# Scores of two attention units in one visit to TensorE, and first output products set ahead of a statistics step

## The chip, the cores and the metric

One core of one Trainium2 chip. The metric is the device time of one execution in microseconds (us). Engines: PE is TensorE (PEld is its weight load), DVE is VectorE, ACT is ScalarE, POOL is GpSimd, SP is SyncE, which issues the DMAs. The granted clock is the share of full speed (2.4 GHz) that TensorE got in a stretch; its other level is 1.2 GHz.

## The reference, cut to what matters

```python
# attention: q, k, v are (4, 8, 576, 64); heads 0-3 see the last 32 positions, heads 4-7 every 32nd position
scores = np.where(masks, q @ k.T / 8, -1e9)
attn = exp(scores - max); attn = attn / (attn.sum() + 1e-9)
x = (attn @ v) reordered to (2304, 512)
# first feed-forward block, with a norm in front
xn = x / sqrt(mean(x * x) + 1e-6) * rms_g
x = (silu(xn @ w_gate) * (xn @ w_val)) @ w_out      # 512 -> 1536 -> 512
# second block
return softplus(x @ w_in) @ w_out2                  # 512 -> 2048 -> 512
```

Everything is float32 outside.

## The kernel before, in words

**Order.** The kernel does not issue its instructions as it meets them. Each is put down with `pr.add(engine, estimated cost, closure, reads, writes)`; a planner (`Program.emit`, `Trial.run`) then lists all of them in an order made from those estimates, the dependencies and due times. `emit` is called twice: once for attention and ten of the twelve steps of block 1's first side, once for the rest. So what the program text gives is dependencies; the order on each engine is the planner's, and an engine then runs its list strictly in that order.

**Attention.** The work is cut in 32 units. A unit is one batch, one pair of heads (p = 0, 1 local, p = 2, 3 strided) and 4 to 6 blocks `a` of queries; two units in a row (u even, u odd) are the two parts of one pair of heads, loaded together (`load`). `stage_s(u)` makes the scores of a unit in one PSUM bank: a bf16 product that writes the mask (L540), then per block and head a 64 by 64 float32 product (L546), 96 columns wide for local units and 54 for strided ones. Head h lies in rows 64h to 64h + 63 of the operands, and its scores go to partitions 64h to 64h + 63 of the bank, so the two heads of a unit use two opposite quarters of the 128 by 128 array: (rows 0-63, columns 0-63) and (rows 64-127, columns 64-127). A float32 product is two PE instructions in the profile. Then VectorE takes the maximum (L558). For units 0 to 15 ScalarE does the exponentials from the bank (L576); for units 16 to 31 VectorE subtracts first (L560) and ScalarE does one exponential (L573). `stage_t` transposes the probabilities (L614), `stage_v` multiplies with the values (L637). There, the two units of a strided pair have their keys in rows 0-53 and 64-117, and their two heads in the two column halves, and `values` puts both units' products down together.

**Units 0 to 15** run in `attend`, with PE, ScalarE and VectorE all at work. The scores have four banks (`q_banks`) up to unit 11; from step 12 (`early`) two (`s_banks`), as `f_banks` then takes the first gate and value products. `at_step(17, prepare, 1, (0,), ...)` starts the preparation of step 1's gate and value weights.

**Units 16 to 31** are dealt out among the steps of block 1 (`steps`, four units at a time, two banks), between the feed-forward products L434.

**Between the two** come, in program order: `half(1, 0)` (gate and value of step 1, tokens 0-511, 24 products), `stats(1)` (sums of squares L453, Ln and Exp L457/L458, three VectorE steps, `norm`), a load of ScalarE's Silu table, `chain1` for (0, 0) and (1, 0) (Silu L844, product L845, a split in two float32r parts L833/L355), `direct(1)` (splits of the normed tokens 512-1023 for the products), and `half(0, 1)`. The first output products `out1` for tokens 0-511 (`outs1(1, True, (0, 1))`, four calls of six products L434 and one ScalarE copy L876) come later, with those for tokens 512-1023, after step 1.

Of the kernel before, what the change touches and what calls it, by code (L numbers as in the profile page):

```python
# [18 lines left out]
EXP_LN = "natural_log_exp_and_others"  # L19
# [6 lines left out]
KD = DM // 128  # L26
# [6 lines left out]
QW = 608  # L33
# [4 lines left out]
DEALT = 10  # L38
# [209 lines left out]
def attn_glu_softplus(  # L248
# [16 lines left out]
    def all_of(key):  # L265
        return (key, 0, 1 << 30)
# [211 lines left out]
    def attention(at, use):  # L478
# [18 lines left out]
        for b in range(B):  # L497
            for p in (0, 2, 1, 3):
                units += [(b, p, 0, 5), (b, p, 5, 4)] if p < 2 else [(b, p, 0, 6), (b, p, 6, 5)]
        probs, trans, vals, ld, both, scored = {}, {}, {}, {}, {}, {}  # L500

        def load(u, b, p, n):
            loc = p < 2
# [17 lines left out]
        def load_v(u):  # L521
# [4 lines left out]
            vals[u // 2] = (vt, kv)  # L526
            dma(nt * (48 if p < 2 else 50), lambda: nc.sync.dma_start(out=vt[:kp, :nt, :], in_=src), [], [all_of(kv)])

        def stage_s(u):
            b, p, t0, n = units[u]  # L530
            loc = p < 2
            nk, st = (LK, 64) if loc else (SK, SK)
            if t0 == 0:
                load(u, b, p, n)
            qt, kq = ld[u // 2]
            sp, kb_ = use.s.next()
            m0 = 64 + ((5 - n) * LK if loc else 5 * LK)
            for h in range(2):
                r = slice(64 * h, 64 * h + 64)
                pr.add("PE", n * nk / 4.8 + 10, lambda r=r: nc.tensor.matmul(  # L540
                    sp[r, :n * nk], lhsT=mask[r, :64], rhs=mask[r, m0:m0 + n * nk], start=True, stop=False,
                    skip_group_check=True), [all_of("mask")], [kb_], mode=3)
            for a in range(n):
                for h in range(2):
                    r, x = slice(64 * h, 64 * h + 64), (t0 + a) * st
                    pr.add("PE", 83 if loc else 54, lambda a=a, h=h, r=r, x=x: nc.tensor.matmul(  # L546
                        sp[r, a * nk:(a + 1) * nk], lhsT=qt[r, x:x + 64], rhs=qt[r, QW + x:QW + x + nk],
                        start=False, stop=True, skip_group_check=True),
                        [(kq, t0 + a, t0 + a + 1), (kq, t0 + a + 100, t0 + a + 101)]
                        + [all_of("id")] * (u == 1), [kb_], mode=3)  # L550
            sv = sp[:, :n * nk].rearrange("p (a c) -> p a c", c=nk)
            e, ke = eb.next()
            e = e[:, :n * nk]
            ev = e.rearrange("p (a c) -> p a c", c=nk)
            z, kz = mz.next()
            m, z = z[:, 0, :n], z[:, 1, :n]
            km, kz = (kz[0], 10, 20), (kz[0], 0, 10)
            dve(n * nk, lambda: nc.vector.reduce_max(out=m, in_=sv, axis=AX.X), [kb_], [km])  # L558
            if whole(u):
                dve(n * nk, lambda: nc.vector.tensor_sub(ev, sv, m.unsqueeze(2).to_broadcast([128, n, nk])),  # L560
                    [kb_, km], [ke])
            else:
                dve(6, lambda: nc.vector.tensor_scalar(out=m, in0=m, scalar1=-SCALE, scalar2=None, op0=ALU.mult),
                    [km], [km])
            scored[u] = (e, ke, ev, z, kz, sv, kb_, m, km)
# [58 lines left out]
        def stage_v(u):  # L624
            b, p, t0, n = units[u]
            loc = p < 2
            r0, r1 = (0, LK) if loc else (64, 64 + SK) if t0 else (0, SK)
            v0 = t0 if loc else 0
            vt, kv = vals[u // 2]
            pts = trans.pop(u)  # L630
            nq = 64 if loc else SK
            xb, kx = use.v.next()
            for a in range(n):
                t, kt = pts[a // 3]
                for h in range(2):
                    o = (2 * (a % 3) + h) * nq
                    pr.add("PE", 59, lambda a=a, h=h, o=o, t=t: nc.tensor.matmul(  # L637
                        xb[64 * h:64 * h + 64, a * nq:(a + 1) * nq], lhsT=vt[r0:r1, v0 + a, 64 * h:64 * h + 64],
                        rhs=t[r0:r1, o:o + nq], start=True, stop=True), [all_of(kv), kt],
                        [kx], mode=1 if loc else 3)  # L640
            g = rg_sb[:, p:p + 1]
            if loc:
                c0 = b * S + 64 * t0
                w = 64 * n
                lo, hi = c0, c0 + w
                src = xb[:, :w]

                def tokens(x, x0, a0, a1):
                    return x[:, a0 - x0:a1 - x0]

                def mine(x, a0, a1):
                    return x[:, a0 - lo:a1 - lo]
            else:
                cls = min(3 * n, 32 - 3 * t0)
                w = cls * 18
                lo, hi = b * S, (b + 1) * S
                src = xb[:, :w].rearrange("p (c m) -> p c m", m=18)

                def tokens(x, x0, a0, a1):
                    return x[:, a0 - x0:a1 - x0].rearrange("p (m c) -> p c m", c=32)[:, 3 * t0:3 * t0 + cls, :]  # L660

                def mine(x, a0, a1):
                    return x[:, :, (a0 - lo) // 32:(a1 - lo) // 32]
            kss = ("ssq", lo, hi)
            for a0, a1 in ((lo, min(hi, TA)), (max(lo, TA), hi)):
                if a0 >= a1:
                    continue
                m = w * (a1 - a0) // (hi - lo)
                y = tokens(sview(a0, a1), a0, a0, a1)
                z = mine(src, a0, a1)  # L670
                kss = ("ssq", a0, a1)
                if a1 <= TA:
                    x, kxs = xview(p, a0, a1)
                    evict(m, tokens(x, a0, a0, a1), z, [kx], [kxs])
                    continue
                if p == 0:
                    act(m, lambda y=y, z=z: nc.scalar.activation(y, z, AF.Square), [kx], [kss])
                else:
                    s2, k2 = sq.next()
                    s2 = s2[:, :m] if loc else s2[:, :m].rearrange("p (c m) -> p c m", m=(a1 - a0) // 32)  # L680
                    act(m, lambda s2=s2, z=z: nc.scalar.activation(s2, z, AF.Square), [kx], [k2])
                    two("POOL", m, "tensor_add", y, y, s2, [kss, k2], [kss])
                x, kxs = xview(p, a0, a1)
                evict(m, tokens(x, a0, a0, a1), z, [kx, all_of("rg")], [kxs], g)
# [270 lines left out]
    with tc.manual_schedule():  # L955
# [6 lines left out]
        def at_step(u, fn, *args):  # L962
            plan.setdefault(u, []).append((fn, args))
# [22 lines left out]

        at_step(HOLD[0] + 3, prepare, 0, (0, 1), HOLD[0])
        at_step(12, early)
        at_step(17, prepare, 1, (0,), HOLD[1])

        def fill(u):
            pr.side = True
# [18 lines left out]

        def side_a(f, queue):

            if f and f != DEALT:
                prep1(f, 0, (0, 1) if f > 1 else (1,))
            w = w_at(f, 0)
            for c in (0, 1) if f > 1 else (1,):
                gate, val = gates.pop((f, c), (None, None))
                gate = gate or plain(w, 0, c, f_banks)
                step(queue)  # L1020
                drain(1)
                val = val or plain(w, 1, c, f_banks)
                step(queue)
                g[f, c] = chain1(gate, val, eng="DVE" if f < DEALT else "POOL")
                drain(1 if f < W1N - 1 else 0)
                step(queue)
            if f % 2:
                todo.extend(outs1(f, f == 1, (0, 1)))

        with ExitStack() as c2:  # L1030
            use = SimpleNamespace(s=q_banks, t=t_banks, v=v_banks)
            x = attention(c2.enter_context(tc.tile_pool(name="at", bufs=1)), use)
            attend(x, fill)
            pr.side = True
            half(1, 0, s_banks)
            pr.side = False
            stats(1, t_banks)
            table("silu_and_others")
            for f in (0, 1):
                g[f, 0] = chain1(*gates.pop((f, 0)))  # L1040
            direct(1)
            half(0, 1, v_banks)
            tv = Ring(banks.t[2:4], "bank", 2)
            use.t = use.v = tv
            for i in (0, 1):
                fk["gv"].keys[len(fk["gv"].t)] = ("ssq", i * CH, i * CH + CH)
                fk["gv"].t.append(ssq[:, i * CH:i * CH + CH])
            queue, last_turn = steps(x, {1: (2,)}, tv)
            o_banks.t = banks.t[4:6]
            for f in range(DEALT):  # L1050
                side_a(f, queue)
            step(queue, len(queue))
            prep1(DEALT, 0)
            pr.emit()
# [131 lines left out]
```

## Time and profile before

| | |
|---|---|
| Median of three runs | 910.92 us (910.21 to 915.23) |
| The profiled execution | 912.66 us, its span 910.9 us |
| PE busy | 893.4 us of the span |
| DVE busy | 717.1 us |
| ACT busy | 484.6 us |
| POOL busy | 21.7 us |
| Granted clock, mean | 0.994 |

The span is the time from the first to the last instruction; the run's own time has 1.8 us more around it. Matmuls are pipelined and overlap, so a busy PE is not a PE at its peak; the distance between the starts of two instructions says what one costs in a row of them.

### The profile page before, as it was taken

How to read it: one execution, taken by the hardware profiler on the slowest of the kernel's cores; microseconds unless marked ns; L12 is line 12 of the kernel's file. 1: busy time of each engine (PE TensorE's matmuls, PEld its weight loads, DVE VectorE, ACT ScalarE, POOL GpSimd, SP SyncE). 2: the span in 40 equal slices, each digit the busy share in tenths (PEclk: the TensorE clock that was granted, in tenths of full speed). 3: DMA queues.
4: the chain of work that ended last, by engine and by line, in shares of the span. 5: the costliest groups of instructions: out<-in, count | busy, mean ns of one | idle time of the engine just before them, and what ended most of it. 6: DMA issues, size and time to landing. Idle time of an engine off the chain costs nothing.

```text
span 910.9 us, 14075 instructions
## 1 busy us (share of the span) xinstructions
PE 893.4 (98%) x5320; PEld 736.5 (81%) x5320; DVE 717.1 (79%) x1358; ACT 484.6 (53%) x992; POOL 21.7 (2%) x22
## 2 busy tenths in 40 slices
PE   8888999999999999999999999999999999999998
PEld 7666787778778788888888888888888888888886
DVE  5979888898589995888988799886699556676645
ACT  6967664535355566545445568544473764343331
POOL 0001000000000000000000000000000000000000
PEclk9999999999999999999999999999999999999999
DMA  8865666262240263345544006331114111101003
GB/s 262 271 190 158 214 196 202 99 193 88 82 128 23 81 196 105 104 139 162 179 145 128 24 24 216 118 104 46 47 47 139 48 47 47 46 24 45 2 1 116
DMA packets 41859, 102.19 MB, mean 112 GB/s; under 512 B 4800, under 2 KB 5568, under 8 KB 41792
## 3 DMA queue, kind: packets, MB, share of 16 engines
q1 hardware_dynamic: 41792, 101.31, 35.1%
q8 instruction: 41, 0.67, 0.3%
q14 instruction: 26, 0.21, 0.1%
HBM read 78.74 MB, written 22.54 MB: 111 GB/s over the span
## 4 chain that ended last, share of the span: by engine, by line
PE 66%; DVE 3%; issue 0%
PE bank L434 66%; DVE xs L878 1%; DVE ob L355 0%; DVE tb L355 0%; DVE xs L355 0%; DVE win L355 0%; DVE w L355 0%; DVE ssq L355 0%; DVE glx L355 0%; DVE xs L896 0%; DVE gv L355 0%; DVE gv L845 0%; DVE ssq L845 0%; DVE gl L355 0%
## 5 line engine op out<-in xcount | busy, mean ns | idle before, releaser
L434 PE MATMUL bank<-ob,win 128*128 128x512 f32 (+1 forms) x1560 | 436.0, 363 | 4.5 <-ACT ob L351 2.5
L434 PEld LDWEIGHTS bank<-ob,win 128*128 128x128 f32 x1560 | 285.7, 189 | 57.9 <-ACT ob L351 2.7
L434 PE MATMUL bank<-tb,win 128*128 128x512 f32 x672 | 232.9, 392 | 0.0
L434 PEld LDWEIGHTS bank<-tb,win 128*128 128x128 f32 x672 | 125.4, 188 | 22.9 <-DVE xs L878 0.4
L896 DVE TENSOR_TENSOR xs<-bank,xs 128x512 f32<-128x512 f32 x126 | 87.0, 691 | 45.6 <-PE bank L434 44.3
L405 ACT ACTIVATE win<-w 128x512 fp32r<-128x512 f32 (+1 forms) x136 | 83.5, 617 | 64.0 <-PE bank L434 37.2
L434 PE MATMUL bank<-wout,ghx 128*128 128x512 f32 x304 | 100.0, 390 | 0.0
L355 DVE TENSOR_TENSOR win<-w,win 128x512 fp32r<-128x512 f32 (+1 forms) x132 | 87.8, 671 | 14.7 <-ACT win L405 11.5
L434 PE MATMUL bank<-wout,gh 128*128 128x512 f32 x272 | 90.4, 390 | 0.0
L434 PE MATMUL bank<-ghx,wout 128*128 128x512 f32 x224 | 84.1, 394 | 0.0
L434 PE MATMUL bank<-gh,wout 128*128 128x512 f32 (+1 forms) x256 | 81.6, 354 | 0.5 <-DVE xs L878 0.4
L878 DVE TENSOR_TENSOR xs<-bank,xs 128x512 f32<-128x512 f32 (+1 forms) x100 | 62.7, 632 | 11.0 <-PE bank L434 10.1
L434 PEld LDWEIGHTS bank<-wout,ghx 128*128 128x128 f32 x304 | 56.9, 188 | 11.7
L434 PEld LDWEIGHTS bank<-wout,gh 128*128 128x128 f32 x272 | 50.9, 188 | 10.5
L793 ACT ACTIVATE gv<-bank 128x512 f32<-128x512 f32 x48 | 28.5, 593 | 47.8 <-PE bank L434 47.2
L434 PE MATMUL bank<-wout,glx 128*128 128x512 f32 x152 | 53.1, 389 | 0.0
L434 PEld LDWEIGHTS bank<-gh,wout 128*128 128x128 f32 x256 | 45.5, 189 | 8.2 <-DVE xs L878 1.4
L434 PEld LDWEIGHTS bank<-ghx,wout 128*128 128x128 f32 x224 | 41.9, 188 | 8.4 <-ACT ghx L833 0.2
L434 PE MATMUL bank<-wout,gl 128*128 128x512 f32 x136 | 47.7, 389 | 0.0
L373 DVE SCALAR_TENSOR_TENSOR cvu<-raw,cvu 128x512 uint32<-128x512 uint32 x68 | 46.8, 688 | 0.9
L355 DVE TENSOR_TENSOR w<-w 128x256 f32<-128x256 f32 x109 | 45.9, 421 | 0.9
L797 DVE TENSOR_TENSOR gv<-bank,gv 128x512 f32<-128x512 f32 x48 | 33.0, 688 | 16.0 <-ACT gv L793 9.0
(128 smaller groups left out, 1238.8 us busy)
## 6 DMA issues: line engine op xcount, KB each, us to landing
raw<-w SPq DMA_DIRECT2D x68, 512.0 KB, 4.1
w<-w_kept SPq DMA_DIRECT2D x56, 256.0 KB, 2.7
w_kept<-cvtx SPq DMA_DIRECT2D x26, 256.0 KB, 4.0
cvt<-w_kept SPq DMA_DIRECT2D x26, 256.0 KB, 2.8
w_kept<-w SPq DMA_DIRECT2D x24, 256.0 KB, 3.8
qk<-qk SPq DMA_DIRECT2D x8, 601.0 KB, 4.4
w_kept<-cvt SPq DMA_DIRECT2D x18, 256.0 KB, 3.4
cvtx<-w_kept SPq DMA_DIRECT2D x18, 256.0 KB, 2.8
```

Source lines behind the costliest of these rows:

```text
L355: pr.add("DVE", 68 + n / 0.96, lambda: getattr(nc.vector, name)(o, x, y), r, w, alt=(110 + n * 2.3, lambda: getattr(nc.gpsimd, name)(o, x, ...
L373: dve(512, lambda: nc.vector.scalar_tensor_tensor(out=u, in0=wlo, scalar=29, in1=u, op0=ALU.logical_shift_right, op1=ALU.bitwise_or), [kra ...
L405: act(n, lambda: nc.scalar.activation(h, t, AF.Copy), [kt], [reg(0, o + lo, o + hi)])
L434: lambda a=a, b=b, i=i, st=st, mv=mv: nc.tensor.matmul(o, lhsT=st[a], rhs=mv[b], start=(first and i == 0), stop=(last and i == m - 1), ski ...
L793: act(CH, lambda: nc.scalar.activation(o, y[0], AF.Copy), [y[1]], [ko])
L797: dve(CH, lambda: nc.vector.tensor_add(o[0], y[0], o[0]), [y[1], o[1]], [o[1]])
L878: dve(n, lambda: nc.vector.tensor_add(x, pb, x), [kp, kx], [kx])
L896: dve(DM, lambda: nc.vector.tensor_add(x, pb, x), [kp, kx], [kx])
```

## The change

- `stage_s` at an even unit now puts down the scores of that unit and the next one together, in two banks, for all units but 12 to 15. Each node of the planner holds the four mask products, or the four products of one block `a` (two heads, two units; two products where only one unit has that block). It needs both banks free and both units' operands.
- A new `half(u, h)` gives the rows of head h and the place of its scores: in odd units the halves are exchanged, so that the four products lie in the four quarters of the array. `stage_v` reads the exchanged halves of odd units back in place.
- The output weights of step 1 are prepared with its gate and value weights (step 17, parts (0, 1)) and no longer in `side_a(1)`.
- After `half(1, 0)` come the Silu table, `chain1` for (0, 0) and (1, 0), the four `out1` for tokens 0-511 on banks 6 and 7, a load of the Exp/Ln table, `stats(1)`, and the Silu table again: two table loads more than before. `side_a(1)` leaves those four `out1` out.

```diff
+        def half(u, h):
+            o = h ^ (u % 2)
+            return slice(64 * h, 64 * h + 64), slice(64 * o, 64 * o + 64)
+
...
-            sp, kb_ = use.s.next()
-            m0 = 64 + ((5 - n) * LK if loc else 5 * LK)
-            for h in range(2):
-                r = slice(64 * h, 64 * h + 64)
-                pr.add("PE", n * nk / 4.8 + 10, lambda r=r: nc.tensor.matmul(
-                    sp[r, :n * nk], lhsT=mask[r, :64], rhs=mask[r, m0:m0 + n * nk], start=True, stop=False,
-                    skip_group_check=True), [all_of("mask")], [kb_], mode=3)
-            for a in range(n):
-                for h in range(2):
-                    r, x = slice(64 * h, 64 * h + 64), (t0 + a) * st
-                    pr.add("PE", 83 if loc else 54, lambda a=a, h=h, r=r, x=x: nc.tensor.matmul(
-                        sp[r, a * nk:(a + 1) * nk], lhsT=qt[r, x:x + 64], rhs=qt[r, QW + x:QW + x + nk],
-                        start=False, stop=True, skip_group_check=True),
-                        [(kq, t0 + a, t0 + a + 1), (kq, t0 + a + 100, t0 + a + 101)]
-                        + [all_of("id")] * (u == 1), [kb_], mode=3)
+            if u % 2 == 0 or not (u >= 16 or u < 12):
+                pair = [u, u + 1] if (u >= 16 or u < 12) else [u]
+                spots = [(x, *units[x][2:], *use.s.next()) for x in pair]
+                for x, _, _, sp, kb_ in spots:
+                    banked[x] = sp, kb_
+                keys = [kb_ for *_, kb_ in spots]
+                n0 = 64 + ((5 - n) * LK if loc else 5 * LK)
+
+                def masked():
+                    for x, t0, n, sp, _ in spots:
+                        m0 = 64 + ((5 - n) * LK if loc else 5 * LK)
+                        for h in range(2):
+                            r, o = half(x, h)
+                            nc.tensor.matmul(
+                                sp[o, :n * nk], lhsT=mask[r, :64], rhs=mask[r, m0:m0 + n * nk], start=True, stop=False,
+                                skip_group_check=True)
+
+                pr.add("PE", n * nk / 2.4 + 15, masked, [all_of("mask")], keys, mode=3)
+                for a in range(n):
+                    here = [s for s in spots if a < s[2]]
+
+                    def scores(a=a, here=here):
+                        for h in range(2):
+                            for x, t0, n, sp, _ in here:
+                                r, o = half(x, h)
+                                c = (t0 + a) * st
+                                nc.tensor.matmul(
+                                    sp[o, a * nk:(a + 1) * nk], lhsT=qt[r, c:c + 64], rhs=qt[r, QW + c:QW + c + nk],
+                                    start=False, stop=True, skip_group_check=True)
+
+                    pr.add("PE", 167 if loc else 116, scores,
+                           [(kq, b0 + a + o, b0 + a + o + 1) for _, b0, *_ in here for o in (0, 100)]
+                           + [all_of("id")] * (u == 1), [k for *_, k in here], mode=3)
+            sp, kb_ = banked.pop(u)
...
-                    o = (2 * (a % 3) + h) * nq
+                    o = (2 * (a % 3) + (h ^ (u % 2))) * nq
...
-        at_step(17, prepare, 1, (0,), HOLD[1])
+        at_step(17, prepare, 1, (0, 1), HOLD[1])
...
-            if f and f != DEALT:
-                prep1(f, 0, (0, 1) if f > 1 else (1,))
+            if f > 1 and f != DEALT:
+                prep1(f, 0)
...
-                todo.extend(outs1(f, f == 1, (0, 1)))
+                todo.extend(outs1(f, f == 1, (0, 1) if f > 1 else (1,)))
...
-            stats(1, t_banks)
             table("silu_and_others")
             for f in (0, 1):
                 g[f, 0] = chain1(*gates.pop((f, 0)))
+            o_banks.t = f_banks.t
+            o_banks.keys = {i: (f"bank{i + 6}", 0, 1 << 20) for i in (0, 1)}
+            pr.side = True
+            for d in range(KD):
+                out1([0, 1], g, True, 0, d)
+            pr.side = False
+            o_banks.keys = {}
+            table(EXP_LN)
+            stats(1, t_banks)
+            table("silu_and_others")
             direct(1)
             half(0, 1, v_banks)
```

## Rows read from the trace of the kernel before

**Rows 1.** The page's first part: busy us, share of the span, instructions.
```profile
PE 893.4 (98%) x5320; PEld 736.5 (81%) x5320; DVE 717.1 (79%) x1358; ACT 484.6 (53%) x992; POOL 21.7 (2%) x22
```

**Rows 2.** Busy time by stretch: length, PE, PEld, DVE, ACT, POOL, granted clock, DMA, GB/s.
```profile
20.00:36.00 16.00, 15.43 (x272) 11.29 (x271) 15.31 (x48) 15.97 (x79) 0.00 (x0) 1.00 0.94 297
...
69.00:74.20 5.20, 1.94 (x20) 1.14 (x18) 5.13 (x10) 4.85 (x8) 0.00 (x0) 1.00 0.31 119
74.20:81.00 6.80, 6.78 (x24) 5.18 (x26) 6.77 (x10) 3.13 (x7) 1.59 (x1) 0.75 0.16 32
81.00:100.00 19.00, 19.00 (x145) 15.52 (x142) 18.70 (x45) 12.93 (x22) 2.86 (x2) 1.00 0.69 222
...
260.00:911.00 651.00, 646.23 (x3124) 542.40 (x3123) 507.43 (x896) 333.31 (x602) 13.14 (x10) 1.00 0.28 89
```

**Rows 3.** Waits of PE from 40 to 81 us: total, times, longest.
```profile
PE bank L540 <- ACT gv L844: 2.6, 1, 2.6
...
PE bank L434 <- DVE ob L355: 0.7, 1, 0.7
```

**Rows 4.** Waits of PE from 81 us to the end.
```profile
PE bank L434 <- DVE xs L878: 0.7, 2, 0.4
```

**Rows 5.** Timeline of PE: the scores of units 24 to 27; start, length, instructions.
```profile
162.73 0.36 PE L540 MATMUL bank<-mask 64*64 64x480 bf16 x1
...
162.94 1.04 PE L546 MATMUL bank<-qk 64*64 64x96 f32 x20
163.76 0.38 PE L540 MATMUL bank<-mask 64*64 64x384 bf16 x2
164.07 0.50 PE L434 MATMUL bank<-glx,wout 128*128 128x512 f32 x1
...
166.48 4.24 PE L434 MATMUL bank<-ob,win 128*128 128x512 f32 x18
170.65 0.88 PE L546 MATMUL bank<-qk 64*64 64x96 f32 x16
171.36 0.30 PE L540 MATMUL bank<-mask 64*64 64x324 bf16 x2
171.50 0.85 PE L546 MATMUL bank<-qk 64*64 64x54 f32 x24
172.28 2.83 PE L434 MATMUL bank<-ob,win 128*128 128x512 f32 x11
175.05 0.30 PE L540 MATMUL bank<-mask 64*64 64x270 bf16 x2
...
175.85 0.50 PE L434 MATMUL bank<-ob,win 128*128 128x512 f32 x1
```

**Rows 6.** Timeline of PE: float32 products that have the array alone.
```profile
60.56 1.88 PE L453 MATMUL bank<-gv,ones 128*128 128x512 f32 x4
...
62.37 0.95 PE L637 MATMUL bank<-pt,vb 54*64 54x54 f32 x44
```

**Rows 7.** Timeline of PE: the value products of a strided pair.
```profile
207.54 0.90 PE L637 MATMUL bank<-pt,vb 54*64 54x54 f32 x40
208.23 0.36 PE L540 MATMUL bank<-mask 64*64 64x480 bf16 x1
```

**Rows 8.** Timeline between attention and block 1, ScalarE and VectorE.
```profile
67.25 0.69 ACT L457 ACTIVATE ssq<-bank,eps 128x512 f32<-128x512 f32 x1 [1.22 <-PE bank L453]
...
68.49 0.69 DVE L355 TENSOR_TENSOR wout<-cvtx,wout 128x512 fp32r<-128x512 f32 x1 [1.09 <-ACT wout L425]
69.08 1.28 ACT L291 ACT_TABLE_LOAD   x1
...
70.95 1.07 ACT L844 ACTIVATE gv<-bank 128x512 f32<-128x512 f32 x2
```

**Rows 9.** Timeline of VectorE: it reads two score banks.
```profile
81.86 1.12 DVE L558 TENSOR_REDUCE mz<-bank 128x5 f32<-128x480 f32 x2
...
82.90 1.11 DVE L560 TENSOR_TENSOR eb<-bank,mz 128x480 f32<-128x480 f32 x2
```

More of the change, by code (lines that the diff above doesn't have):

```diff
@@ L499, in attention @@
                 units += [(b, p, 0, 5), (b, p, 5, 4)] if p < 2 else [(b, p, 0, 6), (b, p, 6, 5)]
-        probs, trans, vals, ld, both, scored = {}, {}, {}, {}, {}, {}
+        probs, trans, vals, ld, both, scored, banked = {}, {}, {}, {}, {}, {}, {}
         def load(u, b, p, n):
```

## The prediction, made before the changed kernel was run

> **What bounds the kernel now.** I read the page first, then the stretches, then the waits of PE, then the timeline where PE stands still and where it makes scores. The page says that PE is busy for 98% of the span [rows 1]. Since a busy PE need not be a full one, the second view cuts the span where the work changes. The reader should see four things in it [rows 2]. While units 4 to 15 pass (20 to 36 us) ScalarE is busy 15.97 of 16 us, and PE, though it shows 15.43, has ScalarE beside it as the bound. From 69 to 74.2 PE works 1.94 of 5.20 us. From 74.2 to 81 PE looks full, but its granted clock is 0.75, so half of that stretch (3.4 of 6.8 us) went at 1.2 GHz, straight after the idle time. From 81 us on PE is full at clock 1.00, to the end.
>
> The waits say the same. Between 40 and 81 us the two that matter here are 2.6 us before the scores of unit 16, for banks that the Silu of step 1 still has to read, and 0.7 us before `half(0, 1)`, for the split tokens of `direct(1)` [rows 3]. After 81 us the longest entry sums to 0.7 us [rows 4]. So behind 81 us what is taken off PE's list comes off the time, as long as the others deliver; ahead of it, only what shortens the idle stretch or the slow clock counts.
>
> **Part 1, scores in four quarters, units 16 to 31.** The timeline of one group of four units (two pairs, one local, one strided) shows three visits [rows 5]: 162.73 to 164.07, 170.65 to 172.28 and 175.05 to 175.85, so 1.34 + 1.63 + 0.80 = 3.77 us. Inside, the 20 instructions of a local unit take 163.76 - 162.94 = 0.82 us, 41 ns each, and 24 strided ones 172.28 - 171.50 = 0.78 us, 32.5 ns each.
>
> Does the array do more than two of them at once? A float32 instruction of 512 columns that has the array alone starts every (62.37 - 60.56) / 4 = 0.45 us [rows 6], or 0.88 ns a column: 85 ns for 96 columns, 48 ns for 54. The local scores at 41 ns are two abreast. The nearest row to the new form is that of the value products of a strided pair: 54 rows by 64 columns, 54 columns wide, from both row halves to both column halves, two units put down together. They start every (208.23 - 207.54) / 40 = 17.2 ns [rows 7], where two abreast could not go under 24 ns. So more than two quarters work at once there, and I take this row for strided steps, and half of 41 ns for local ones.
>
> The new price of a group: the local pair is 0.21 us of masks (162.94 - 162.73, taken for four products as now for two), four steps of eight instructions at 20.5 ns (0.164 us each) and a last step with one unit, four at 41 ns (0.164 us): 1.03 us. The strided pair is 0.14 us of masks (171.50 - 171.36), five steps of eight at 17.2 ns (0.138 us each) and a last one of four at 32.5 ns (0.13 us): 0.96 us. Together 1.99 us, so 3.77 - 1.99 = 1.78 us less, and 7.1 us in four groups. Bounds: 0 if the quarters take turns; at best, four quite abreast (12 ns an instruction in the strided steps), 0.96 falls to 0.72 and the sum is 8.1 us. I take 7.1, as the form of [rows 7] differs from the new one in little but which bank each quarter writes.
>
> The value products leave one thing untested: each of their banks is filled from one row half. In the new scores the two quarters that fill one bank come from different row halves. But so do the two heads of a unit now, and they run two abreast (41 against 85 ns) [rows 5, 6]. The Trainium skill, "TensorEngine Tiling (Array Packing)", Restrictions and Gotchas, says that different row tiles cannot access the same PSUM bank at the same time; by it each bank's two quarters would take turns, at most two would run abreast as now, and part 1 would bring nothing. This case's trace disagrees for two quarters, at 41 ns; for four it is open, and it is a rival below.
>
> **Part 1, units 0 to 11.** Six pairs, some 5 us less for PE, hidden behind ScalarE [rows 2]: 0. If that cover were gone, it would be a gain. Against it, the maximum of the even unit waits for the odd one's scores, under 1 us, and the first pair waits for both parts of its load. Four banks cover the first, the second comes once: from -1 to +1, taken as 0. The exchanged halves cost nothing: VectorE and ScalarE work on all 128 partitions as before, and `stage_v` only reads other columns.
>
> **Part 2, `wout` of step 1 at step 17.** The planner had already put it ahead of its place in the text: its last split ends at 68.49 + 0.69 = 69.18 us [rows 8]. Its DMA and its four VectorE steps are the same in number; 0. It sets when the moved products can end: half of their terms need it.
>
> **Part 3, output products ahead of `stats(1)`.** Moved are 24 products. A product of 512 columns costs (170.65 - 166.48) / 18 = 0.232 us [rows 5], so 5.6 us of PE. They don't vanish, they go where PE stands: 2.6 + 0.7 us of waits [rows 3], and if PE stays busy there, the 1.7 us that 3.4 us at 1.2 GHz lose [rows 2] come back too: 5.0 us at most. With the Silu table ahead, the banks of step 1 come free earlier, so the first score pair (1.03 us) fits in as well. The work suffices; `wout` at 69.2 us is just in time.
>
> What it adds: two table loads of 1.28 us on ScalarE, and an order. Silu now starts before Ln; the second Exp/Ln table waits for the Silu of step 1, Ln of `stats(1)` waits for that table, and behind Ln stand Exp, three VectorE steps, `norm`, `direct(1)` and `half(0, 1)`. Ln began at 67.25 after 1.22 us of idle ScalarE, and the gate of step 1 can be made earlier than it was. So one load is hidden there, and the other replaces the one at 69.08 [rows 8]. But ScalarE is busy 4.85 of 5.20 us and VectorE 5.13 of 5.20 in just that stretch, and VectorE 18.70 of 19 us behind it [rows 2]: PE can be ahead only as far as VectorE is. The products and splits of `chain1` move forward with it, which helps. Ends: a gain of 5.0 us; a loss of 2.6 us, both loads on the path. I take a gain of 3.
>
> **Sum.** 7.1 + 0 + 0 + 3.0 = 10.1 us off. From the profiled execution's 912.66 us this gives 902.6 (its span 910.9 to 900.8); that execution is 1.7 us above the median of 910.92, so for the median 901.
>
> **Rivals.**
>
> *The gap is not closed.* The planner orders by its own due times, and may leave the 24 products behind the statistics, or the second Exp/Ln table comes late. For it: ScalarE's full stretch. Against: the text now forces Silu first, and the products are then ready. It leaves 7.1 us: 904; with both table loads on the path, 7.1 - 2.6 = 4.5: 906.4.
>
> *The quarters take turns*, so the change doesn't do what it says. For it: no row shows this use of the banks with four; against: 17.2 ns. Then only the 3 us are left: 908, no measurable change. What speaks for it by the page is told above.
>
> *Slower: the pair holds both banks.* Units 16 to 31 have two score banks. Now the next unit can start when one is read; a pair needs both. Reading two banks takes VectorE 1.12 + 1.11 = 2.23 us [rows 9], behind its other work, and PE's list is fixed, so if the planner puts a pair too early, all products behind it wait. For it: VectorE without slack from 69 to 100 us [rows 2]. Against: 0.7 us of such waits in all now [rows 4], and the planner knows the banks. One wait of 2.23 us in each of four groups eats 8.9 of the 10.1 us: 909.7. It decides from (10.1 + 4.6) / 4 = 3.7 us a group on; at 5 us, 921.
>
> **Chances.** Three runs spread over 0.5%, so about 4.6 us (0.5%) is what can be told from no change. As forecast 0.52 (own range 897.5 to 904). Gap not closed 0.22: 0.17 of it faster, 0.05 the same. Turns 0.08: the same. Banks held 0.18: 0.08 the same, 0.10 slower. So faster 0.69, same 0.21, slower 0.10. The range, 896 to 909.5, takes in the first two cases, the turns and the lower part of the third; about 0.18 is left out, mostly above.
>
> **What the profile after would show.** Right: score instructions of 54 columns about 17 ns apart and of 96 about 20; two visits a group, of about 1 us each; no granted clock under 1.00 between 69 and 81 us; `out1` products there; PE full by about 74 us; waits of PE after that still under 2 us. Wrong if the pitch stays at 32 to 41 ns (turns), if PE shows waits before L540's masks for VectorE (banks held), if Ln of `stats(1)` starts later than some 69 us, with PE idle behind it, or if the clock falls in attention, where PE has less to do, so that ScalarE is no longer the bound there.

## The result, and the profile after

The changed kernel takes 900.21 us (median of 4 runs, 899.77 to 900.53) against 911.21 of the kernel before: a ratio of 0.987, 95% interval 0.984 to 0.990. Run once more beside the last experiments it took 901.46 against 911.57: 0.989 (0.987 to 0.990). The forecast was 901, its range 896 to 909.5. The profiled execution took 900.52 us, its span 898.7, which is 12.2 us less than that of before.

The stretches of [rows 2], of the kernel after (length, PE, PEld, DVE, ACT, POOL, granted clock, DMA, GB/s):

```profile
20.00:36.00 16.00, 14.32 (x266) 10.49 (x267) 14.02 (x41) 14.88 (x76) 0.00 (x0) 0.90 0.94 305
...
69.00:74.20 5.20, 4.75 (x28) 3.17 (x28) 3.37 (x6) 3.96 (x7) 0.00 (x0) 1.00 0.47 150
74.20:81.00 6.80, 6.41 (x52) 4.88 (x52) 6.76 (x12) 4.51 (x9) 0.00 (x0) 1.00 0.29 100
81.00:100.00 19.00, 19.00 (x132) 15.07 (x130) 18.63 (x44) 14.35 (x24) 1.29 (x1) 1.00 0.62 182
```

From 69 to 74.2 us PE now works 4.75 us where it worked 1.94, and from 74.2 to 81 the granted clock is 1.00 where it was 0.75. How far ahead that puts PE is read by counting its products. The instructions of L434 up to 81 us, first before, then after (columns: length, PE busy and count, PEld, clock, DMA, GB/s):

```profile
0.00:81.00 81.00, 22.19 (x70) 14.62 (x70) 0.94 0.67 215
```

```profile
0.00:81.00 81.00, 24.36 (x91) 16.44 (x92) 0.94 0.71 230
```

By 81 us 91 products have started where it was 70: 21 more, at 0.232 us [rows 5] 4.9 us.

The scores of units 24 to 27, timeline of PE in the kernel after (start, length, instructions; the answer to [rows 5]):

```profile
153.98 0.36 PE L553 MATMUL bank<-mask 64*64 64x480 bf16 x1
...
154.15 1.08 PE L566 MATMUL bank<-qk 64*64 64x96 f32 x36
155.16 0.50 PE L434 MATMUL bank<-glx,wout 128*128 128x512 f32 x1
...
165.61 0.33 PE L553 MATMUL bank<-mask 64*64 64x324 bf16 x4
165.75 0.87 PE L566 MATMUL bank<-qk 64*64 64x54 f32 x44
166.55 0.73 PE L434 MATMUL bank<-ob,win 128*128 128x512 f32 x2
```

Two visits in place of three, 1.18 and 0.94 us: 2.12 us a group, where it was 3.77. The strided instructions come every (166.55 - 165.75) / 44 = 18.2 ns, the local ones every (155.16 - 154.15) / 36 = 28 ns. These are means over a visit, up to the start of the next product. Inside a visit the distance is smaller. Each pair of lines here is the timeline of one visit cut off at two times 0.41 us apart (154.24 and 154.65 us, 165.86 and 166.27 us), so that the counts tell how many instructions started in between:

```profile
154.15 0.32 PE L566 MATMUL bank<-qk 64*64 64x96 f32 x4
154.15 0.74 PE L566 MATMUL bank<-qk 64*64 64x96 f32 x24
...
165.75 0.32 PE L566 MATMUL bank<-qk 64*64 64x54 f32 x9
165.75 0.73 PE L566 MATMUL bank<-qk 64*64 64x54 f32 x37
```

Four abreast start every 0.41 / 20 = 20.5 ns (local) and 0.41 / 28 = 14.6 ns (strided). The rest of the mean is the last step with two abreast, and the way from the last score instruction to the first product of L434: 154.98 to 155.16 us and 166.40 to 166.55 us, some 0.17 and 0.15 us.

Four groups give 4 x 1.65 = 6.6 us, and with the 4.9 us of lead that is 11.5 of the 12.2 us.

What happens ahead of the products, timeline of ScalarE after (to [rows 8]):

```profile
57.28 1.28 ACT L291 ACT_TABLE_LOAD   x1
...
59.16 0.61 ACT L867 ACTIVATE gv<-bank 128x512 f32<-128x512 f32 x1
...
62.52 1.28 ACT L291 ACT_TABLE_LOAD   x1
...
70.76 0.69 ACT L457 ACTIVATE ssq<-bank,eps 128x512 f32<-128x512 f32 x1 [1.22 <-PE bank L453]
...
73.05 1.28 ACT L291 ACT_TABLE_LOAD   x1
```

Silu comes at 59.16 us, where it came at 70.95. The table goes back to Exp/Ln at 62.52, long before Ln, so Ln doesn't wait for it: its line says that it waits for the sums of PE. Yet Ln starts 3.5 us later than before (70.76 against 67.25). PE's list explains it: between the last transposes and the last value products of attention, which the sums need, it does twelve gate and value products and five output products, and reaches those value products only at 65.63 us instead of 62.37 [rows 6]. That delay cost nothing that the products did not fill.

The waits of PE from 75 us to the end, after (total, times, longest; to [rows 4]):

```profile
PE bank L434 <- DVE xs L901: 0.6, 2, 0.4
PE bank L434 <- ACT ob L351: 0.4, 1, 0.4
PE bank L637 <- DVE xs L279: 0.2, 1, 0.2
```

No wait before a mask: the pairs, which need both banks, hold up nothing.

### The profile page after: what moved, and what is told of

It is laid out like the page before. It is cut to its first block, busy times and chain, and to the rows that moved or that the text cites. A ratio compares the mean times of both kernels' runs of the same rounds, so it can differ in the third digit from the quotient of the medians.

```text
span 898.7 us, 14075 instructions
## 1 busy us (share of the span) xinstructions
PE 882.7 (98%) x5320; PEld 725.7 (81%) x5320; DVE 712.9 (79%) x1349; ACT 486.1 (54%) x999; POOL 28.1 (3%) x26
## 4 chain that ended last, share of the span: by engine, by line
PE 67%; DVE 3%; issue 0%
PE bank L434 67%; DVE xs L901 1%; DVE ob L355 0%; DVE tb L355 0%; DVE xs L355 0%; DVE win L355 0%; DVE w L355 0%; DVE ssq L355 0%; DVE glx L355 0%; DVE xs L919 0%; DVE gv L355 0%; DVE ssq L868 0%; DVE gv L868 0%; DVE gl L355 0%
## 5 line engine op out<-in xcount | busy, mean ns | idle before, releaser
L434 PE MATMUL bank<-ob,win 128*128 128x512 f32 (+1 forms) x1560 | 430.8, 360 | 2.7 <-ACT ob L351 1.8
L434 PEld LDWEIGHTS bank<-ob,win 128*128 128x128 f32 x1560 | 283.4, 188 | 55.0 <-ACT ob L351 2.2
L434 PE MATMUL bank<-tb,win 128*128 128x512 f32 x672 | 232.8, 392 | 0.0
L434 PEld LDWEIGHTS bank<-tb,win 128*128 128x128 f32 x672 | 125.4, 188 | 22.9 <-DVE xs L901 0.4
L434 PE MATMUL bank<-wout,ghx 128*128 128x512 f32 x304 | 100.0, 390 | 0.0
L434 PE MATMUL bank<-wout,gh 128*128 128x512 f32 x272 | 90.4, 390 | 0.0
L434 PE MATMUL bank<-ghx,wout 128*128 128x512 f32 x224 | 84.1, 394 | 0.0
L434 PE MATMUL bank<-gh,wout 128*128 128x512 f32 (+1 forms) x256 | 81.3, 356 | 0.5 <-DVE xs L901 0.4
L434 PEld LDWEIGHTS bank<-wout,ghx 128*128 128x128 f32 x304 | 56.9, 188 | 11.7
L434 PEld LDWEIGHTS bank<-wout,gh 128*128 128x128 f32 x272 | 50.9, 188 | 10.6
L434 PE MATMUL bank<-wout,glx 128*128 128x512 f32 x152 | 53.2, 389 | 0.0
L434 PEld LDWEIGHTS bank<-gh,wout 128*128 128x128 f32 x256 | 45.5, 189 | 9.0 <-DVE xs L901 1.4
L434 PEld LDWEIGHTS bank<-ghx,wout 128*128 128x128 f32 x224 | 41.9, 188 | 8.4 <-ACT ghx L856 0.2
L434 PE MATMUL bank<-wout,gl 128*128 128x512 f32 x136 | 47.7, 389 | 0.0
```

The costliest lines, as they stand in the source:

```text
L434: lambda a=a, b=b, i=i, st=st, mv=mv: nc.tensor.matmul(o, lhsT=st[a], rhs=mv[b], start=(first and i == 0), stop=(last and i == m - 1), ski ...
```

## The experiments

Each kernel was run beside the kernel before on the same chip; all times are medians.

| kernel | us | before | ratio (95%) |
|---|---|---|---|
| changed | 900.2 | 911.2 | 0.987 (0.984 to 0.990) |
| changed, again | 901.5 | 911.6 | 0.989 (0.987 to 0.990) |
| scores only | 908.3 | 912.3 | 0.996 (0.994 to 0.998) |
| output products first only | 909.3 | 912.3 | 0.997 (0.996 to 0.998) |
| two quarters | 908.5 | 912.3 | 0.996 (0.995 to 0.997) |
| unit by unit | 900.0 | 912.3 | 0.987 (0.985 to 0.989) |
| pairs from unit 16 | 902.0 | 912.7 | 0.988 (0.986 to 0.990) |
| scores only, from unit 16 | 909.7 | 912.7 | 0.995 (0.994 to 0.997) |
| output weights late | 901.5 | 912.7 | 0.987 (0.985 to 0.989) |
| statistics first | 909.1 | 912.7 | 0.997 (0.995 to 0.998) |
| scores only, first pair single | 908.1 | 911.6 | 0.996 (0.995 to 0.997) |
| measured costs | 905.0 | 911.6 | 0.992 (0.991 to 0.994) |
| output products first, copies on ScalarE | 904.3 | 911.6 | 0.992 (0.991 to 0.994) |

### Two quarters

```diff
         def half(u, h):
-            o = h ^ (u % 2)
+            o = h
...
-                    o = (2 * (a % 3) + (h ^ (u % 2))) * nq
+                    o = (2 * (a % 3) + h) * nq
```

> The whole change, but head h of every unit keeps its own half, so that the four products of a step lie in two quarters; the planner's costs, and so the order of every engine, are those of the changed kernel. Theory (the array works in four quarters at once): score instructions go back from 28 to about 42 ns (local) and from 18 to about 32 ns (strided), 1.5 us in each of four groups: 6 us over the changed kernel, 906. Rival (the gain is in the joined visits and the planner's new order): 900 to 901.

This is the cleanest of the comparisons, as all engines keep the order of the changed kernel. It took 908.5 us, 7 to 8 us more than the changed kernel: the direction expected, and more than the 6 us. Timeline of PE, same units:

```profile
157.97 1.70 PE L566 MATMUL bank<-qk 64*64 64x96 f32 x36
159.61 0.50 PE L434 MATMUL bank<-glx,wout 128*128 128x512 f32 x1
...
170.31 1.49 PE L566 MATMUL bank<-qk 64*64 64x54 f32 x44
171.73 0.74 PE L434 MATMUL bank<-ob,win 128*128 128x512 f32 x2
```

In the mean over a visit this is 45.6 and 32.3 ns an instruction, against 28 and 18.2. Inside the visits, cut off 0.41 us apart as above (at 158.06 and 158.47 us, 170.42 and 170.83 us):

```profile
157.97 0.32 PE L566 MATMUL bank<-qk 64*64 64x96 f32 x3
157.97 0.74 PE L566 MATMUL bank<-qk 64*64 64x96 f32 x13
...
170.31 0.32 PE L566 MATMUL bank<-qk 64*64 64x54 f32 x5
170.31 0.73 PE L566 MATMUL bank<-qk 64*64 64x54 f32 x19
```

41 and 29.3 ns, against 20.5 and 14.6: in the same 0.41 us four quarters start twice as many. So the array does work in four quarters at once, also where the two quarters of one bank come from different row halves. Joining the visits alone is worth little: this kernel's 908.5 us stand beside the 909.3 of the output products alone, where each unit is scored by itself (and the order is another).

In the score instructions the difference is 0.63 + 0.62 = 1.25 us a group, with the masks 1.58. Between the profiled executions this kernel is 1.2 us behind at the first mask of unit 16 (73.04 against 71.81 us) and 6.6 us at the end, so some 5.4 us fall behind that mask and 1.2 ahead of it. Against the execution of "unit by unit" below, whose clock is the same as here in every stretch up to 81 us, it is 3.2 us at that mask and 8.6 at the end.

Ahead of it only the pairs of units 0 to 11 differ. The same 200 or so instructions of PE, from the scores of units 2 and 3 on, in the second execution of the changed kernel, in this kernel, and in the first execution of the changed kernel (columns as in [rows 2]):

```profile
18.61:25.65 7.04, 6.43 (x200) 5.29 (x196) 6.83 (x24) 6.52 (x37) 0.00 (x0) 1.00 0.75 242
```

```profile
18.77:27.25 8.48, 8.22 (x200) 7.18 (x196) 7.21 (x24) 6.54 (x38) 0.00 (x0) 1.00 0.65 192
```

```profile
17.38:25.99 8.61, 8.61 (x198) 7.42 (x196) 6.63 (x23) 6.10 (x34) 0.00 (x0) 0.66 0.67 206
```

At the same clock two quarters take 1.4 us longer here, with PE busy 8.22 of 8.48 us and ScalarE 6.54. From there to the first mask of unit 16 all three take 45.8 us, so this loss is not hidden: it moves the end of attention.

### Unit by unit

```diff
-                        for h in range(2):
-                            for x, t0, n, sp, _ in here:
+                        for x, t0, n, sp, _ in here:
+                            for h in range(2):
```

> The whole change, but inside a step the two products of one unit come one after the other, then those of the next unit: the row half alternates with each product, where the changed kernel has two of one row half in a row. Local steps measured 26 ns an instruction where 20.5 were forecast. Theory A (two in a row from one row half hold each other up): local instructions at 20 to 22 ns, 0.2 us less a group, 899 to 900. Theory B (four abreast cost what they cost): 26 ns, 900, no difference. Rival (two quarters of one bank in a row hold each other up): over 30 ns, 901 to 903.

900.0 us, and the same means of 28 and 18.2 ns. As theory B has it, the order within a step doesn't matter. But the 26 ns from which the expectation starts is a mean with the way to the next product in it: inside the steps both kernels go at 20.5 ns, so there was nothing to win.

### Scores only, and output products first only

The first is the changed kernel with `stats(1)`, `outs1` and `prepare(1, (0,))` back in their old places; the second the kernel before with these three changed and the scores left alone.

> Only the scores in pairs and four quarters; statistics 1, the output products and the output weights stand where they stood before. Theory (two gains that add up): 6 to 7.5 us off, about 904 to 905, with the idle time of PE before the scores of unit 16 (2.6 us) and the slow clock behind it (0.75 in some 7 us) still there. Rival (one gain: the scores only paid because the other edit let PE run ahead): under 3 us off, 908 or more. Rival (the output products paid nothing): 900.

> Only the output products of tokens 0-511 and the Silu table ahead of statistics 1, and the output weights at step 17; the scores as before. Theory: the 5.0 us by which PE was ahead at 81 us come from here: 4 to 5 us off, 906 to 907, no granted clock under 1.00 between 69 and 81 us. Rival (the idle time closed because the score pair fits there): 1 to 2 us off, 909 to 910. Rival (the two added table loads are paid without the scores' slack): no gain, 911.

908.3 and 909.3 us: 4.0 and 3.1 us off, 7.1 together, where both at once give 10 to 12. The two gains don't add up; neither theory had that. Two places show where they went. In the first, the gap stays: timeline of PE, then the stretch behind it.

```profile
67.86 1.49 PE L434 MATMUL bank<-ob,win 128*128 128x512 f32 x4
74.17 8.09 PE L434 MATMUL bank<-ob,win 128*128 128x512 f32 x24 [4.82 <-ACT ob L351]
```

```profile
74.20:81.00 6.80, 6.80 (x20) 5.23 (x21) 6.80 (x12) 3.68 (x6) 0.00 (x0) 0.64 0.10 10
```

PE waits 4.8 us in one piece, and the clock is 0.64 behind it, worse than the 0.75 before. In the second, PE is ahead at 81 us by 17 products (87 against 70) and by 60 score instructions against 14, and its span ends only 3.4 us ahead. Waits of its weight loads from 81 to 260 us:

```profile
PEld bank L614 <- DVE xs L279: 3.0, 6, 0.7
...
PEld bank L434 <- DVE gv L845: 1.4, 1, 1.4
```

In the kernel before the first of these was 0.8 us and the second not listed. PE ran ahead and then waited for VectorE.

### Output products first, copies on ScalarE

Beside the edits of the output-products-first kernel (`flex=False` keeps a copy off VectorE):

```diff
-    def evict(n, o, x, r, w, scale=None, cost=0):
+    def evict(n, o, x, r, w, scale=None, cost=0, flex=True):
...
-            o, x, AF.Copy, scale=1.0 if scale is None else scale), r, w, alt=(66 + n / 0.96, on_dve))
+            o, x, AF.Copy, scale=1.0 if scale is None else scale), r, w, alt=(66 + n / 0.96, on_dve) if flex else None)
...
-                evict(m, tokens(x, a0, a0, a1), z, [kx, all_of("rg")], [kxs], g)
+                evict(m, tokens(x, a0, a0, a1), z, [kx, all_of("rg")], [kxs], g, flex=False)
```

> Only the output products and the Silu table ahead (the kernel that took 909.3), with the scaled copies of attention's outputs kept on ScalarE and off VectorE. In the 909.3 kernel PE was about 6 us ahead at 81 us, scores counted, and ended 3.4 us ahead; its weight loads before transposes waited 3.0 us for these copies on VectorE. Theory (the lead was given back to VectorE): those waits go, and 1.5 to 2.5 us come off, 907 to 908. Rival (the waits only move to ScalarE or to other work of VectorE): 909 to 910.

904.3 us, 5.0 less than without the edit; no wait of the weight loads for VectorE between 81 and 260 us is left in the list. The direction was right and the size twice the expected: 98 products stood at 81 us, eleven more than without the edit (and 24 score instructions fewer), so attention gained too. This fits a lead that was given back to VectorE, with more to be had there. It doesn't show it alone, since the edit also changed the planner's order on every engine.

### Scores only, first pair single

Units 16 and 17 one by one, the rest as in the scores-only kernel.

> Only the scores, as in the kernel that took 908.3, but units 16 and 17 one by one; pairs from unit 18 on and for units 0 to 11. In the 908.3 kernel PE stood 4.8 us without a break until the splits of tokens 512-1023, at a clock of 0.64 behind it, where the kernel before broke the wait (2.6 and 0.7 us) with the scores of unit 16. Theory (a pair needs both score banks, and one of them is not free until the Silu and its product are through, so the pair cannot go into the gap): unit 16 is back in the gap, the waits sum to 3.5 us or less, and 1 us or more comes back although one pair is given up: 907 or less. Rival (the longer wait has nothing to do with the pair): 908.3 plus the 0.8 us of the pair given up, 909.

Timeline of PE:

```profile
73.22 0.61 PE L553 MATMUL bank<-mask 64*64 64x480 bf16 x2 [3.92 <-ACT gv L867]
```

Unit 16 is back in the gap and the wait is 3.9 us instead of 4.8, but the time is 908.1: the 0.9 us are about what giving up a pair costs, and the clock behind the wait is 0.64 as before. The pair giving up its place in the gap does not explain why the scores alone bring 4 us; that theory fell.

### Statistics first

The changed kernel with `stats(1, t_banks)` ahead of the first Silu table, and neither the Exp/Ln nor the second Silu load behind `out1`.

> The whole change, but statistics 1 stand again ahead of the Silu table, so that the two added table loads fall away; the output products follow the Silu and stand ahead of the splits of tokens 512-1023. Theory (what closes the gap is that Silu, and with it the products, no longer wait for Ln and Exp): the idle time and the slow clock come back, 4 to 5 us, 904 to 905. Rival (the place of the products in the text is enough and the loads are a cost): 898 to 900.

909.1 us, some 8 us more, about twice what the theory expected, and the largest effect of a few lines. Timeline of PE:

```profile
76.00 1.22 PE L434 MATMUL bank<-gh,wout 128*128 128x512 f32 x2 [6.10 <-ACT gh L856]
```

Silu, and with it the output products, waits for Ln and Exp again, and PE stands for 6.1 us. The two added table loads are what buys the products their place.

### Pairs from unit 16, with and without the output products ahead

```diff
-            if u % 2 == 0 or not (u >= 16 or u < 12):
-                pair = [u, u + 1] if (u >= 16 or u < 12) else [u]
+            if u % 2 == 0 or not u >= 16:
+                pair = [u, u + 1] if u >= 16 else [u]
```

> The whole change, but only units 16 to 31 are scored in pairs; units 0 to 11 go one by one, as 12 to 15 do. Theory of the prediction (what units 0 to 11 save is hidden behind ScalarE): no difference to the changed kernel, 899.5 to 901. Rival (with PE's gap closed, attention's end is on the path and the quarters shorten attention): 902 to 904. Rival (pairs lower the clock in attention and cost more than they save): 897 to 899.

> Only the scores in pairs, and only those of units 16 to 31; statistics 1, the output products and the output weights stand where they stood before. The scores alone with all pairs took 908.3, 4 us off. Theory (the four groups give some 5 to 6 us behind 81 us, and the pairs of units 0 to 11 in that kernel brought attention nothing or a later end): 906 to 907. Rival (the four groups themselves give only 4 us without the output products ahead): 908. Rival (the pairs of units 0 to 11 carried part of the gain): 909 to 911.

902.0 and 909.7 us, with intervals that overlap those of the kernels with all pairs (0.988 beside 0.987 and 0.989; 0.995 beside 0.996). So what units 0 to 11 bring is 2 us at most and by these medians not told from nothing. But both times lie where the rivals put them that let the pairs of units 0 to 11 carry a part (902 to 904, 909 to 911), and with the order kept, in two quarters, a loss of 1.4 us is seen in just these pairs. So the rivals are the likelier here, and the cover by ScalarE is not complete.

### Output weights late

`prep1(1, 0, (1,))` right before `out1`, and part (0,) alone at step 17.

> The whole change, but the output weights of step 1 are put down right before the output products that need them and not at step 17. Theory (the planner already had them early): no difference to the changed kernel, 899.5 to 901. Rival (the early place is what lets the products fill the gap): 2 us or more later, 902 to 905.

901.5 us: no difference.

### Measured costs

```diff
-                    pr.add("PE", 167 if loc else 116, scores,
+                    pr.add("PE", 215 if loc else 146, scores,
```

> The whole change, with the planner's cost of a step set to what was measured: 215 ns (local, was 167) and 146 ns (strided, was 116). Theory (PE's list has slack for the others, so a better estimate changes little): 899 to 901. Rival (PE ran ahead of its plan, and waits come from that): 897 to 899.

905.0 us: 3.5 to 5 us slower with the same instructions. Both expectations were wrong. The new costs are nearer to a whole visit up to the next product (5 x 215 ns = 1.08 and 6 x 146 ns = 0.88 us, measured 1.01 and 0.80) than the old ones (0.84 and 0.70 us), but a step itself, eight instructions at 20.5 or 14.6 ns, takes 164 or 117 ns, as the planner already had it. The stretch from the start to 81 us, instructions of L434, and PE's wait in the timeline:

```profile
0.00:81.00 81.00, 24.83 (x83) 16.02 (x84) 0.92 0.72 230
```

```profile
78.23 4.05 PE L434 MATMUL bank<-ob,win 128*128 128x512 f32 x15 [1.85 <-ACT ob L351]
```

Here 83 products have started by 81 us, 8 fewer than in the changed kernel, and `half(0, 1)` starts at 78.23 us, not at 76.55. The planner made another order, and by 81 us 8 products, 1.9 us, are lost.

### The changed kernel again

> The changed kernel once more, beside the others on this chip: 899.5 to 901 if the first runs were typical.

901.5 us, half a us above the expected, and 93 products at 81 us: the first runs were at the lower end.

## Why the prediction was right

*What bounds the kernel.* As read: PE full behind 81 us, idle and slowly clocked before. A later `half(0, 1)` (76.55 against 74.22 us) cost nothing, since PE had other work.

*Scores in four quarters.* 7.1 us forecast, 6.6 found in the visits. The mechanism is as told: two quarters against four, with the order kept, give half the distance, 41 to 20.5 ns (local) and 29.3 to 14.6 (strided). So the forecast's 20.5 ns was exact. What its price of the local pair left out is the way from the last score instruction to the next product, some 0.17 us: the pair's 36 took 1.01 us where 0.82 was forecast, while in [rows 5] a mask followed on the 20 local instructions that gave the 41 ns. The strided pair came out as forecast (0.80 us for 0.82) partly by luck: its instructions go at 14.6 ns and not 17.2, which about pays for the 0.15 us behind its last one. The 32.5 ns of [rows 5] were a mean with that way in it.

The rival of quarters that take turns is out. If the two quarters of each bank took turns, only two instructions could be at work; a lone one of 54 columns takes 48 ns by the prediction's working, so four would need 96 ns, and they take 59 (0.41 / 7 us). For these instructions the trace so disagrees with the Trainium skill's rule that different row tiles cannot access the same PSUM bank at the same time, "TensorEngine Tiling (Array Packing)", Restrictions and Gotchas.

*Units 0 to 11: 0.* Between 0 and 2 us, not told apart by the medians. The reason given, that ScalarE hides what PE saves there, does not hold throughout: the two-quarter form lost 1.4 us in these pairs, and the loss reached the end of attention. The clock did fall there in the profiled execution (0.90 from 20 to 36 us), as the last paragraph of the forecast feared. The stretch shown above took 8.61 us at clock 0.66 and 7.04 in the second execution of the same kernel at 1.00, so the fall cost 1.6 us in that execution. It doesn't come with the change: the second execution has 1.00 from 20 to 36 us.

*`wout` at step 17: 0.* So it was.

*Output products first: 3 taken, up to 5.0.* 4.9 us of lead at 81 us: nearly the whole of the upper bound. The 2 us kept back for table loads and for VectorE were not lost in the whole change: the loads lay off Ln's path, the slow clock and the wait for banks went, and of the 3.3 us in which PE was not busy from 69 to 81 us 0.8 are left.

*The sum.* 10.1 forecast, 11.0 and 10.1 measured in the medians, 12.2 in the profiled spans. But the sum took for granted that its two terms stand apart, and they don't: alone they brought 4.0 and 3.1 us, and each takes some 7 to 9 us with it when it is left out. So the total is right, and in part by luck: no run confirms its split in 7.1 and 3.0.

Shown is that the scores alone leave a wait of 4.8 us (3.3 before) and a slower clock behind it in place. The wait is 1.5 us longer, and the clock loses (0.75 - 0.64) x 6.8 = 0.7 us more, an estimate from the two stretches: 2.2 of the 2.6 us that are missing from 6.6. For the products alone it is shown that the weight loads wait longer for VectorE (3.0 and 1.4 us, where it was 0.8). That these waits took the lead is likely and not shown apart. Why the whole change escapes them (1.1 us before transposes where it was 3.0) is not settled: every edit also gives the planner another problem, and another order of the same instructions was worth 3.5 to 5 us with the measured costs.

*Banks held.* The rival on the other side did not come: no wait before a mask.

## What to carry to other kernels

Price a new way to use the array from the distance inside a run of such instructions, and price the way to the next product apart: halving the 41 ns of two abreast was exact, and what was missing was the 0.15 to 0.17 us behind the last one. A mean over a visit mixes the two. Idle time of the bounding engine that is followed by a slow clock is worth more than its length, and work that only lacks an early operand (here Silu, held by a table order) is what to put there. Where a planner orders the work, an edit made alone does not show that edit's share; keep the order and change only the instruction's form, and expect several us from the order itself. When counting work up to a time, use one stretch: an instruction that lies across the border of two is counted in both.

## What the runs showed of the hardware

Four float32 products of 64 by 64, one in each quarter, two banks: one instruction every 14.6 ns at 54 columns and every 20.5 ns at 96, against 29.3 and 41 ns in two quarters. So four quarters did twice the work in the same time at both widths. From the last score instruction to the next product of the whole array it was 0.15 us at 54 columns and 0.17 at 96, with two quarters as with four. The order of row halves within a step made no difference.
